# Transposing K, Q and memory rows in four 32-wide column tiles instead of one 128-wide tile

## The chip, the cores and the metric

The kernel runs on one core of a Trainium2 chip. The metric is the device time of one execution in microseconds; the figure for the kernel before is the median of 3 runs. A profile of one further execution shows where the time goes.

## What is computed

The output has two halves side by side. The left half (A) is a long convolution along the sequence, done with Fourier matrices. The right half (B), which takes most of the time and is where the change is, is attention with a recurrent memory. Cut to what matters:

```
mem = mem0                                   # 8 rows x 1024
for s in range(64):                          # 64 segments, one after the other
    h = concat(mem, x[32 rows of segment s]) # 40 rows x 1024
    q, k, v = h @ Wq, h @ Wk, h @ Wv         # 32 heads x 128 each
    p = softmax(mask(q k^T / sqrt(128)))     # 40 x 40 per head
    o = (p v) @ Wo                           # 40 rows x 1024
    mem = o[:8]                              # goes into the next segment
    out[s] = o[8:]
```

The memory rows of one segment are an input of the next, so the segments cannot overlap on the path through `mem`.

## The kernel before, in words

**Stages.** Up to about 450 us the kernel does half A, and beside it everything of B that does not depend on the memory. From then on it runs the 64 segments (loop at L884); one takes 22.5 us. Those 64 segments are the stage that the change touches.

**Weights.** Wk, Wq, Wv and Wo are cut into 64 chunks of 128 x 2048 bf16 (512 KB). 47 of them stay in SBUF. The other 17 (`STREAM`, L22) are read again from DRAM (tensor `WS`) in each segment, through a ring of tiles named `wring`. From the second segment on, one of the 17 is held in spare PSUM columns and is not read again, and of a second one only 192 KB are read (`KEPT`, L23). That leaves 15 full reads and one short one a segment. `done(ch)` (L834) gives a ring tile back when the last matmul that reads it has been written into the program, and `fetch()` (L716) issues the next read on SP's queue, at L724 or, for the short one, L721. A read waits until the tile it overwrites has been used; six ring tiles are in rotation.

**Order on TensorE.** The order is written out by hand (`tc.manual_schedule()`, L867); each engine works in program order. In one segment, L1020 to L1079:

- `fill_mem(hT, Y, 0)`, then half of the projection K of head group 0; `fill_mem(hT, Y, 1)`, then its other half. `Y` is the output of the segment before, as 128 x 512; `fill_mem` (L859) turns two 128 x 128 blocks of it on TensorE (L862) into PSUM, and VectorE copies the 8 memory columns of each from there into `hT` (L863), which is the weight operand of all projections.
- six projections (K, Q of group 0; K, Q of group 1; V of both groups), each as two calls of `Proj.run(4)`. One `run(4)` is 16 matmuls at L918: for each of four chunks, four matmuls with a 32-column weight (`hT`, 128 x 32) and 512 moving columns, at `tile_position=(0, 32*c)`. The four stand side by side in the array, each with 32 of its columns. After its second `run(4)` the sum is copied from PSUM to SBUF as bf16 by ScalarE (`evac`, L927, tile `qkv_sb`).
- `transposes(sb)` (L930) for K and Q of each group, four calls a segment (L1027, L1031, L1038, L1043). Each turns the four 128 x 128 blocks of `qkv_sb` (L933) into PSUM tile `tps`; VectorE copies the result for group 0, ScalarE for group 1. Each call stands between two `run(4)`, so that 16 projection matmuls lie between an `evac` and the transposes that read it; for the call of L1038, `scores(0)` lies there too.
- `scores` (L936): 32 matmuls with a 32-column weight and 40 moving columns each (L939, L942); softmax on VectorE and ScalarE; `attend` (L976) in 32-row tiles (L980, L984); `out_proj` (L1006) in 64-column tiles (L1002) into `yacc`.
- two ScalarE copies of `yacc` into the next `Y` (L1078), and two stores of its rows on POOL's queue (L1080).

"Tile form" below means the part of the array a matmul uses, as the profile prints it before the shapes: 128\*128 for the whole array, 128\*32 for a column tile of the projections and scores, 32\*128 for attend, 128\*64 for the output projection.

Of the kernel before, what the change touches and what calls it, by code (L numbers as in the profile page):

```python
# [416 lines left out]
def b_kernel(ctx: ExitStack, tc, x, mem0, Wq, Wk, Wv, Wo, outb, n_seg, run_a):  # L417
    nc = tc.nc
# [57 lines left out]
    ident = const.tile([128, 128], BF, name="ident")  # L476
# [262 lines left out]
    with c0p:  # L739
# [16 lines left out]
        for g in range(2):  # L756
# [3 lines left out]
            for tb in range(4):  # L760
                vst = vsts[:, tb] if g == 0 else pair()[:].rearrange("p (c w) -> p c w", c=4)
                for c in range(4):
                    ps = ps0.tile([128, 512], F32, tag="ps0", name="vb_ps")
                    for kc in range(8):
                        nc.tensor.matmul(ps[:], lhsT=xbt(kc)[:, 16 * tb:16 * tb + 16, :].rearrange("p s t -> p (s t)"),  # L765
                                         rhs=ws[kc][:, c * 512:(c + 1) * 512], start=(kc == 0), stop=(kc == 7))
# [87 lines left out]
    def load_x(s):  # L854
        rec = one.tile([128, 768], BF, tag="rec", name="rec")
        nc.gpsimd.dma_start(rec[:], REC[:, s, :])  # L856
        pend[s] = (rec[:, 0:256].rearrange("p (k t) -> p k t", k=8), rec[:, 256:512], rec[:, 512:768])

    def fill_mem(hT, Y, half):  # L859
        tp = tps[:, 0, :]  # L860
        for j in (2 * half, 2 * half + 1):
            nc.tensor.transpose(tp[:, j * 128:(j + 1) * 128], Y[:, j * 128:(j + 1) * 128], ident[:])  # L862
        nc.vector.tensor_copy(  # L863
            hT.rearrange("p (dh j) t -> p dh j t", dh=2)[:, :, 2 * half:2 * half + 2, 0:NM],
            tp.rearrange("p (j dh r) -> p dh j r", j=4, dh=2)[:, :, 2 * half:2 * half + 2, 0:NM])

    with tc.manual_schedule():  # L867
# [3 lines left out]
        Y = one.tile([128, 512], BF, tag="PT", name="Y0")  # L871
# [12 lines left out]
        for s in range(n_seg):  # L884
# [45 lines left out]
            def transposes(sb):  # L930
                tp = tps[:, 0, :]
                for i in range(4):
                    nc.tensor.transpose(tp[:, i * 128:(i + 1) * 128], sb[:, i * 128:(i + 1) * 128], ident[:])  # L933
                return tp.rearrange("p (i c r) -> p i c r", i=4, c=4)

            def scores(g, QT, KT):  # L936
# [79 lines left out]
            def out_quarter(q, w):  # L1016
                hp = [ch[1] for ch in kept if kept[ch] == "A"][0]
                project(2 * hp + q // 2, w, OT1)

            fill_mem(hT, Y, 0)  # L1020
            k0 = Proj(0, 0).run(4)
            fill_mem(hT, Y, 1)
            k0 = k0.run(4).evac()
            q0 = Proj(1, 0).run(4)
            KT0 = keys(0)
            last_queries(0)
            nc.vector.tensor_copy(KT0[:, :, :, 0:32], transposes(k0))  # L1027
            q0 = q0.run(4).evac()
            k1 = Proj(0, 1).run(4)
            QT0 = one.tile([128, 4, 4, 32], BF, tag="QT", name="QT")  # L1030
            nc.vector.tensor_copy(QT0[:], transposes(q0))  # L1031
            k1 = k1.run(4).evac()
            scores(0, QT0, KT0)
            E0 = softmax_a()
            q1 = Proj(1, 1).run(4)
            KT1 = keys(1)
            last_queries(1)
            nc.scalar.copy(KT1[:, :, :, 0:32], transposes(k1))  # L1038
            PT0 = softmax_b(E0)
            q1 = q1.run(4).evac()  # L1040
# [35 lines left out]
            Y = one.tile([128, 512], BF, tag="PT", name="Y")  # L1076
# [8 lines left out]
def kernel(  # L1085
# [27 lines left out]
    with ExitStack() as ctx_b:  # L1113
        b_kernel(ctx_b, tc, B_x[0], B_mem0[0],
                 B_Wq.rearrange("d h e -> d (h e)"), B_Wk.rearrange("d h e -> d (h e)"),
                 B_Wv.rearrange("d h e -> d (h e)"), B_Wo.rearrange("h e d -> (h e) d"),
                 outb, n_seg, run_a)
# [35 lines left out]
```

## Time and profile before

| | us |
|---|---|
| median of 3 runs (1904.03 to 1904.1) | 1904.04 |
| the profiled execution's own time | 1907.36 |
| its span, first to last instruction | 1905.6 |
| one segment, from the chain of waits | 22.51 |

| engine | busy in the span | share |
|---|---|---|
| TensorE matmuls (PE) | 1749.0 us, 26353 instructions | 92% |
| TensorE weight loads (PEld), beside the matmuls | 831.1 us, 26353 | 44% |
| VectorE (DVE) | 853.8 us | 45% |
| ScalarE (ACT) | 674.8 us | 35% |
| GpSimd (POOL) | 342.8 us | 18% |

How to read it: matmuls are pipelined, so the duration of one (380 ns for 512 columns) is longer than the time to the start of the next, and what a matmul costs is read from the starts. A number such as L933 is a line of the kernel. "x1024" counts instructions, and `out<-in` names the tile written and the tiles read. A wait is put down to the instruction whose semaphore ended it.

The transposes are 1024 matmuls at L933 and 256 at L862, each with 128 weight columns (the data) and 128 moving columns (the identity).

### The profile page before, as it was taken

Reading aid. Unit: us, or ns where it says so; the run is one execution under the profiler, and the core shown is the slowest. Engines: PE = TensorE matmul, PEld = TensorE weight load, DVE = VectorE, ACT = ScalarE, POOL = GpSimd, SP = SyncE. Lnnn points to the kernel's source line nnn. Section 1 sums busy time; section 2 is a strip of 40 time slices with the busy share of each in tenths; the row PEclk is TensorE's granted clock in tenths of the full one; section 3 lists DMA queues with packets and bytes.
Section 4 is the critical chain, followed back from the end, with each engine's and each line's share of the span. In section 5 each row is a group of like instructions: output and inputs, shape, how many; then the busy total and the mean of one; then the engine's idle time right before and its main releaser. Section 6 shows DMA issues by size and latency. Waiting matters only on the chain.

```text
span 1905.6 us, 62245 instructions
## 1 busy us (share of the span) xinstructions
PE 1749.0 (92%) x26353; PEld 831.1 (44%) x26353; DVE 853.8 (45%) x2812; ACT 674.8 (35%) x1195; POOL 342.8 (18%) x1014
## 2 busy tenths in 40 slices
PE   6989986778999999999999999999999999999998
PEld 3433322333444444444444444444444444444444
DVE  9927863202344444444444444444443444444443
ACT  6945640112333333333333333333333333333333
POOL 4003341000121111111121111111111111111111
PEclk9999998989999999999999999999999999999999
DMA  9989889998999999999999999999999999999998
GB/s 338 351 302 329 291 271 333 327 284 277 349 373 374 373 378 373 377 372 373 373 373 378 373 376 372 370 372 372 379 374 369 371 378 374 375 373 371 372 379 311
DMA packets 251211, 678.00 MB, mean 356 GB/s; under 512 B 74850, under 2 KB 82930, under 8 KB 250932
## 3 DMA queue, kind: packets, MB, share of 16 engines
q1 hardware_dynamic: 178692, 604.26, 85.0%
q0 software_dynamic: 17488, 46.70, 7.0%
q10 hardware_dynamic: 54752, 23.07, 4.5%
q8 instruction: 206, 3.38, 0.7%
q14 instruction: 73, 0.60, 0.1%
HBM read 618.35 MB, written 59.24 MB: 356 GB/s over the span
## 4 chain that ended last, share of the span: by engine, by line
PE 80%; DMA 7%; DVE 5%; issue 4%; ACT 2%; POOL 0%; ACTq 0%; SPq 0%; DVEq 0%; POOLq 0%
PE acc L918 38%; PE yacc L1002 22%; PE kb_ps L625 5%; PE tps L933 4%; DMA wring<-WS 3%; PE vb_ps L765 3%; DMA REC<-stage 2%; PE OTp L980 1%; ACT s_sb L243 1%; DVE rec L863 1%; PE SB L942 1%; PE tps L862 1%; PE s_ps L241 1%; DMA REC<-xt 1%; PE SB L939 1%
## 5 line engine op out<-in xcount | busy, mean ns | idle before, releaser
L918 PEld LDWEIGHTS <-rec 128*32 128x32 bf16 x12288 | 283.6, 96 | 300.2 <-DVE rec L863 60.7
L927 ACT CAST qkv_sb<-acc 128x512 bf16<-128x512 f32 x384 | 224.7, 585 | 480.0 <-PE acc L918 287.9
L1002 PEld LDWEIGHTS <-OT 128*64 128x64 bf16 x4348 | 255.1, 109 | 195.3 <-ACT OT L992 27.6
L918 PE MATMUL acc<-wring,rec 128*32 128x512 bf16 x2556 | 252.7, 382 | 22.8 <-DVE rec L863 19.1
L918 PE MATMUL acc<-Wres,rec 128*32 128x512 bf16 x3328 | 249.4, 380 | 0.6 <-issue 0.6
L1002 PE MATMUL yacc<-wring,OT 128*64 128x512 bf16 (+1 forms) x1540 | 235.9, 380 | 5.0 <-DMA wring<-WS 4.9
L918 PE MATMUL acc<-Wmid,rec 128*32 128x512 bf16 x3072 | 234.4, 382 | 0.0
L1002 PE MATMUL yacc<-Wmore,OT 128*64 128x512 bf16 (+1 forms) x1280 | 185.4, 381 | 0.0
L817 DVE TENSOR_SCALAR quarter<-OTp 128x256 int32<-128x256 int32 x252 | 101.1, 422 | 187.6 <-ACT OT L992 149.3
L1080 POOL DMA_DIRECT2D out_dram<-Y x128 | 63.7, 502 | 484.5 <-ACT Y L1078 484.2
L918 PE MATMUL acc<-pw,rec 128*32 128x512 bf16 x1796 | 144.8, 382 | 0.1
L1078 ACT CAST Y<-yacc 128x256 bf16<-128x256 f32 x128 | 41.4, 375 | 274.5 <-PE yacc L1002 274.5
L992 ACT CAST OT<-OTp 128x640 bf16<-128x640 f32 x128 | 88.6, 692 | 129.7 <-PE OTp L984 129.0
L918 PE MATMUL acc<-Wlate,rec 128*32 128x512 bf16 x1280 | 104.0, 384 | 17.1 <-DVE rec L863 17.1
L948 DVE TENSOR_REDUCE mx<-SB 128x5 f32<-128x200 f32 x128 | 47.1, 368 | 153.4 <-PE SB L942 153.3
L856 POOL DMA_DIRECT2D rec<-REC x64 | 36.2, 566 | 405.0 <-PE acc L918 372.1
L1002 PE MATMUL yacc<-Wlate,OT 128*64 128x512 bf16 x768 | 105.7, 383 | 0.2 <-ACT OT L992 0.2
L933 PEld LDWEIGHTS <-qkv_sb 128*128 128x128 bf16 x1024 | 57.8, 97 | 109.5 <-ACT qkv_sb L927 108.0
L933 PE MATMUL tps<-ident,qkv_sb 128*128 128x128 bf16 x1024 | 101.6, 222 | 0.4 <-ACT qkv_sb L927 0.3
L893 POOL COPY KT<-rec 128x128 bf16<-128x128 bf16 x128 | 38.2, 298 | 329.4 <-PE SB L942 324.2
L863 DVE COPY rec<-tps 128x32 bf16<-128x32 bf16 x128 | 22.3, 175 | 165.1 <-PE tps L862 115.8
L1027 DVE COPY KT<-tps 128x512 bf16<-128x512 bf16 x64 | 27.1, 424 | 152.2 <-PE tps L933 152.2
(215 smaller groups left out, 2392.9 us busy)
## 6 DMA issues: line engine op xcount, KB each, us to landing
wring<-WS SPq DMA_DIRECT2D x961, 512.0 KB, 6.0
rec<-REC POOLq DMA_DIRECT2D x64, 192.0 KB, 5.8
wring<-WS SPq DMA_DIRECT2D x63, 192.0 KB
SK<-s_sb SPq DMA_DIRECT2D x16, 512.0 KB, 4.8
SU<-s_sb SPq DMA_DIRECT2D x16, 512.0 KB, 4.9
Kg<-SK SPq DMA_DIRECT2D x32, 256.0 KB, 4.2
Ug<-SU SPq DMA_DIRECT2D x32, 256.0 KB, 5.7
REC<-stage ACTq DMA_DIRECT2D x16, 512.0 KB, 10.9
```

The costliest lines, as they stand in the source:

```text
L625: nc.tensor.matmul(ps[:], lhsT=ws[kc][:, hl * 128:(hl + 1) * 128], rhs=xbt(kc).rearrange("p s t -> p (s t)"), start=(kc == 0), stop=(kc == 7))
L765: nc.tensor.matmul(ps[:], lhsT=xbt(kc)[:, 16 * tb:16 * tb + 16, :].rearrange("p s t -> p (s t)"), rhs=ws[kc][:, c * 512:(c + 1) * 512], st ...
L817: nc.vector.tensor_scalar(out=t[:].bitcast(I32), in0=OTi[:, q, 160:416], scalar1=0, scalar2=None, op0=ALU.bitwise_or)
L863: nc.vector.tensor_copy(hT.rearrange("p (dh j) t -> p dh j t", dh=2)[:, :, 2 * half:2 * half + 2, 0:NM], tp.rearrange("p (j dh r) -> p dh ...
L918: nc.tensor.matmul(self.acc[32 * c:32 * c + 32, x - 512 * c:y - 512 * c], lhsT=hT[:, kc, :], rhs=r, start=(n_kc == 0 and x == 512 * c), st ...
L927: nc.scalar.copy(sb[:], self.acc[:])
L933: nc.tensor.transpose(tp[:, i * 128:(i + 1) * 128], sb[:, i * 128:(i + 1) * 128], ident[:])
L948: nc.vector.tensor_reduce(out=mx[:], in_=S, op=ALU.max, axis=AX.X)
L992: nc.scalar.copy(OT[:], o_view)
L1002: nc.tensor.matmul(yacc[64 * dh:64 * dh + m, x - o:y - o], lhsT=lhsT, rhs=r, start=(h == 0 and x == o), stop=(h >= 30), tile_position=(0, ...
L1078: nc.scalar.copy(Y[:, 256 * half:256 * half + 256], yacc[:, 256 * half:256 * half + 256])
L1080: nc.gpsimd.dma_start(bass.AP(outb.tensor, outb.offset + SEG * s * 2048 + 512 * dh, [[2048, 32], [1, 512]]), Y[64 * dh + NM:64 * dh + 40, :])
```

## The change

A helper `turn_tile` replaces each 128 x 128 transpose by four matmuls in transpose mode. Each takes 32 columns of the source as its weight, the whole identity as the moving operand, and writes 32 partitions of the result, at `tile_position=(0, e)`. Both places that transposed in the segment loop call it. Nothing else changes: the order on the other engines and the waits of the first instruction of each group are those of before.

```diff
+    def turn_tile(dst, src):
+        for e in range(0, 128, 32):
+            nc.tensor.matmul(dst[e:e + 32, :], lhsT=src[:, e:e + 32], rhs=ident[:], start=True, stop=True,
+                             is_transpose=True, tile_position=(0, e))
+
     def fill_mem(hT, Y, half):
         tp = tps[:, 0, :]
         for j in (2 * half, 2 * half + 1):
-            nc.tensor.transpose(tp[:, j * 128:(j + 1) * 128], Y[:, j * 128:(j + 1) * 128], ident[:])
+            turn_tile(tp[:, j * 128:(j + 1) * 128], Y[:, j * 128:(j + 1) * 128])
...
             def transposes(sb):
                 tp = tps[:, 0, :]
                 for i in range(4):
-                    nc.tensor.transpose(tp[:, i * 128:(i + 1) * 128], sb[:, i * 128:(i + 1) * 128], ident[:])
+                    turn_tile(tp[:, i * 128:(i + 1) * 128], sb[:, i * 128:(i + 1) * 128])
```

TensorE's 1280 transposes become 5120, each with its own weight load: 3840 more matmuls and 3840 more loads.

## The prediction

> **What bounds the kernel now.** I read the chain of waits first. In a segment it is TensorE almost from end to end; around one call of `transposes` it reads (start us, us, what):
>
> ```profile
> 1002.16 1.84 PE acc L918 x32
> 1004.00 0.33 PE tps L933 x4
> 1004.33 0.98 PE acc L918 x16
> ```
>
> So the transposes lie on the path, and a nanosecond saved on them is one on TensorE's path. What they really cost is read from starts. The timeline of another such call (start us, duration, engine, line, names, tile form and shapes; in brackets the idle time before and what ended it):
>
> ```profile
> 1001.06 0.58 ACT L927 CAST qkv_sb<-acc 128x512 bf16<-128x512 f32 x1 [3.10 <-issue]
> 1001.22 0.39 PE L918 MATMUL acc<-wring,rec 128*32 128x512 bf16 x4
> 1001.44 0.39 PE L918 MATMUL acc<-Wmid,rec 128*32 128x512 bf16 x4
> 1001.66 0.32 SPq L724 DMA_DIRECT2D wring<-WS  x1
> 1001.76 0.23 PEld L933 LDWEIGHTS <-qkv_sb 128*128 128x128 bf16 x4 [0.42 <-ACT qkv_sb L927]
> 1001.76 0.40 PE L933 MATMUL tps<-ident,qkv_sb 128*128 128x128 bf16 x4
> ...
> 1002.09 0.62 PE L918 MATMUL acc<-Wmid,rec 128*32 128x512 bf16 x8
> ```
>
> A group of four projection tiles starts 0.22 us after the one before (1001.22, 1001.44), but the first transpose starts 0.32 us after the last group. From the trace's stamps, the last projection matmul to the first transpose is 312 ns at the median of all 256 calls, against 215 inside a 512-column stream: 97 ns lost. The four transposes then start over 178 ns, and the next projection follows the last of them by 149 ns where transposes follow each other by 56: 93 ns lost. The first projection group after it takes 226 ns instead of 215: 11 more. Is this the change of tile form or the transpose itself? Two places answer. In the first stage a 128\*128 transpose is followed by a 128\*128 matmul:
>
> ```profile
> 278.29 0.23 PE L600 MATMUL xt_ps<-ident,X_sb 128*128 128x128 bf16 x1
> 278.36 0.59 PE L625 MATMUL kb_ps<-XBT,Wmid 128*128 128x512 bf16 x2
> ```
>
> Only 0.07 us lies between them. And the scores, in the same 128\*32 form as the projections, follow them without a loss:
>
> ```profile
> 1004.70 0.60 PE L918 MATMUL acc<-Wmid,rec 128*32 128x512 bf16 x8
> 1005.13 0.19 PE L939 MATMUL SB<-KT,QT 128*32 128x40 bf16 x4
> 1005.16 0.19 PE L942 MATMUL SB<-KT,QBm 128*32 128x40 bf16 x4
> ...
> 1005.38 0.41 PE L918 MATMUL acc<-pw,rec 128*32 128x512 bf16 x4
> ```
>
> 1004.70 to 1005.13 is two groups of 0.215 and nothing else, while the step into `attend` and those into the output projection, other forms, show 309 to 312 ns again. So the loss belongs to the change of form.
>
> The second thing to read is the DMA, from 500 to 1890 us: the rate in 40 equal slices, the queues' share of 16 engines' time, the ring's reads (count, size, median us to landing).
>
> ```profile
> GB/s 379 371 380 373 371 375 375 376 375 379 365 380 369 378 372 377 369 375 378 366 376 375 376 364 384 368 383 359 378 373 377 372 377 375 369 379 363 382 372 381
> ...
> q1 hardware_dynamic: 141904, 496.38, 95.0%
> q0 software_dynamic: 9856, 20.14, 4.3%
> ...
> wring<-WS SPq DMA_DIRECT2D x923, 512.0 KB, 6.0
> ```
>
> The queues add to 100% with the two instruction queues (1.1%). Yet TensorE hardly waits for it; its waits in that window (total us, times, longest):
>
> ```profile
> PE acc L918 <- DMA wring<-WS: 2.3, 4, 0.7
> ...
> PE yacc L1002 <- DMA wring<-WS: 0.3, 1, 0.3
> PE tps L933 <- ACT qkv_sb L927: 0.3, 2, 0.2
> ```
>
> 2.6 us in 1390. So TensorE sets the pace with the DMA close behind: of 939 reads whose landing and use can be paired in the trace, the median lands 1.97 us before its first matmul, one in ten less than 0.9, one in twenty less than 0.63.
>
> **The change, part by part.**
>
> *The transposes themselves.* The trace has no transpose in a column tile. The lower bound of four tiles on a 128 x 128 block is the stream of 128 columns side by side, 56 ns, as one 128-wide transpose now; nothing excludes that they run one after another, 4 x 56 = 224 ns. Rows near it: four projection tiles take 215 ns for 512 columns, which is one stream and not four; four score tiles, each with its own load, take 26 ns for 40 columns (32 in about 0.25 us). A form and column count between these rows, so I take 56 ns, and the 16 of a call 224 ns. Keep 224 a block for the range.
>
> *The loads.* Each tile brings a load. In the scores, 32 loads and 32 matmuls pass in 0.25 us, under 8 ns a pair, less than the 14 that 56/4 leaves. Cost: nothing, hidden behind the streams.
>
> [...]
>
> *Leaving a call.* From the first transpose to the next projection is now 178 + 149 = 327 ns, plus 11: 338. In one form it is 224. Saved 114, four times a segment: 456 ns.
>
> *Entering a call.* 97 ns go, but what is late next is `qkv_sb`. ScalarE's copy ends 115 ns before the first transpose for K of group 0 and 104 before both Qs; the shortest step from a ScalarE copy to a waiting matmul in this trace is 55 ns (Y at L1078 to L862). So these calls gain 60, 49 and 49. K of group 1 has `scores(0)` in front, its data is 377 ns early, and it gains the whole 97. Sum 255 ns.
>
> *Q of group 1 and the scores.* Leaving earlier brings the scores nearer to ScalarE's copy of QT: its end is now 181 ns ahead of them. Leaving gains 107 + 11 = 118, which leaves 63, still over 55. Cost nothing, with 8 ns of cover. The copies of group 0 on VectorE are shorter (424 against 587 ns) and have more.
>
> *`fill_mem`.* The first half waits for Y and then for VectorE: last transpose to projection is 542 ns, nearly all latency, and the form change hides in it: nothing. The second half enters from a projection with 312 ns and its data ready: 97 saved, and 10 on the spacing of the two (66 against 56); its exit waits for VectorE as before. 107 ns.
>
> Sum for TensorE: 456 + 255 + 107 = 818 ns a segment, 64 times: 52 us.
>
> *What the DMA gives back.* No part of the change touches its bytes: 374 GB/s x 22.515 us = 8.42 MB a segment. In 21.70 us that needs 388 GB/s. Two bounds. Above: no slice of the 40 (35 us each) is over 384; at 384 a segment takes 21.93 us, 0.585 less than now, 37 us in all. Below: shares that add to 100% say it is full already, and all 52 us turn into waits at L918 for `wring`. Against the lower end: reads land 1.97 us early, and over single segments the rate goes from 362 to 389. Against the upper: 389 is what the ring reaches when it catches up, and each read needs the slowest of 16 engines; in the median read the first engine lands after 3.8 us and the last after 6.0, so a thin margin is used up often. Neither row is nearer; I take the middle, 19 us, and keep both ends. Instruction fetch grows by 7680 instructions beside TensorE's 52706: at most 15% of that 1.1%, 0.16% of the DMA, some 3 us if the DMA is full, within this term.
>
> Sum: 1907.4 of the profiled execution less 19 is 1888.4; it lies 3.3 us above the median of the runs, so **1885 us**. The 52 us are found again as 33 us of waits for `wring`.
>
> **Rivals.**
>
> 1. *The DMA keeps up; all 52 us are kept*: 1904 − 52 = 1852. For it: 2.6 us of waits now and the 1.97 us of slack. Against it: 388 GB/s asked for over all segments.
> 2. *The DMA is full; nothing moves*: within 4 us of 1904. For it the 100%; then the waits for `wring` come to some 50 us.
> 3. *Slower: the four transpose tiles don't run side by side.* The place is L933 and L862 in every segment. Serial tiles cost 168 ns more a block, 20 blocks: 3.36 us, less 0.82, is 2.54 us a segment or 163 us: 2067 if whole. It decides from the spacing of a block: 818/20 = 41 ns above 56, so from about 97 ns a block the kernel is slower than before. Against it the projections and scores, which are side by side; for it only that transposes in this form occur nowhere.
> 4. *The change doesn't do what it says*: transpose mode beside plain matmuls in the 128\*32 form stalls as well. Then entering and leaving stay at 312 and 149 and the time is that of rival 2. Against it: 278.29 to 278.36 above.
>
> **How the numbers follow.** Partial gain (1862 to 1899): 0.55. Rival 1: 0.15. Rivals 2 and 4: 0.12. Rival 3: 0.18. The range leaves out rival 3, the top of 2 and the bottom of 1: 1850 to 1906, about 8 in 10. Faster by over 0.2%, about what a measurement of this kernel can tell from no change (1900.2), is partial gain and rival 1: 0.70; within it 0.12; slower 0.18.
>
> **What would show it.** Right: L933 and L862 in the 128\*32 form, a block every 56 ns; the step from L918 into a call 216 ns for K of group 1 and about 265 for the others; out of it under 60. The transposes' part of the chain falls from 0.33 to about 0.22 us a call. The DMA rate rises to about 379, and the ring's slack falls well below 1.97 us. Wrong: a block at 100 ns or more (rival 3); steps still at 312 and 149 (rival 4); waits for `wring` that stay at a few us (rival 1) or eat all (rival 2). The sum is wrong in its least certain term if the DMA's margin isn't near 0.3 us a segment.

## The result, and the profile after

| | us |
|---|---|
| before, median of 4 runs (1904.03 to 1908.61) | 1904.07 |
| after, median of 4 runs (1952.67 to 1959.26) | 1955.97 |
| ratio after / before, 95% interval | 1.0267 [1.0243, 1.0290] |
| forecast | 1885, range 1850 to 1906 |

The changed kernel is 52 us slower, and the forecast said 19 us faster. The granted TensorE clock was the same: 0.982 of full speed in the profiled execution of before, 0.982 to 0.984 in the four of after. The lines of the changed kernel have moved: the transposes are now at L861, the projections at L923, the scores at L944 and L947, attend at L985 and L989, the output projection at L1007.

The page of after: the span, the busy time of each engine, the queue that carries instructions (packets, MB, share of the DMA), and the chain of waits by engine.

```profile
span 1953.6 us, 69893 instructions
...
PE 1713.4 (88%) x30161; PEld 849.5 (43%) x30193; DVE 854.9 (44%) x2812; ACT 671.5 (34%) x1195; POOL 344.6 (18%) x1014
...
q8 instruction: 236, 3.87, 0.8%
...
PE 76%; issue 9%; DMA 7%; DVE 4%; ACT 2%; POOL 1%; ACTq 0%; SPq 0%; POOLq 0%; DVEq 0%
```

The two matching lines on the page of before:

```profile
q8 instruction: 206, 3.38, 0.7%
...
PE 80%; DMA 7%; DVE 5%; issue 4%; ACT 2%; POOL 0%; ACTq 0%; SPq 0%; DVEq 0%; POOLq 0%
```

TensorE is busy for less time than before (1713 against 1749 us), and its share of the chain falls. What grew is "issue", from 4 to 9%: time in which an engine stood still and waited for nothing that the profile shows.

**The transposes became as cheap as forecast.** The timeline of TensorE around one call that met no disturbance (start us, duration, engine, line, operation, names, tile form, shapes):

```profile
1043.95 0.40 PE L923 MATMUL acc<-pw,rec 128*32 128x512 bf16 x4
1044.16 0.41 PE L861 MATMUL tps<-ident,qkv_sb 128*32 128x128 bf16 x16
1044.39 0.40 PE L923 MATMUL acc<-pw,rec 128*32 128x512 bf16 x4
```

The call begins 0.21 us after the last group of projections, the ordinary step inside a stream, and the next projection follows its first transpose by 0.23 us, where before it was 0.327. The spacing of blocks, read from the stamps, is 56 ns at the median, as with the 128-wide transpose.

**The loss stands elsewhere, as holes.** The chain of waits of after through the next call (start us, us, what):

```profile
1043.46 0.89 PE acc L923 x16
1044.35 0.22 PE tps L861 x16
1044.57 1.73 PE acc L923 x32
1046.30 0.10 PE tps L861 x2
1046.40 0.85 issue
1047.25 0.40 PE tps L861 x14
```

The call at 1044.35 is whole. The one at 1046.30 stops after two of its 16 transposes, stands for 0.85 us, and goes on. No semaphore is waited for in the middle of a call. The waits of TensorE in the segment stage of after, from 500 to 1940 us (total us, times, longest):

```profile
PE acc L923 <- DVE rec L868: 37.7, 122, 0.3
PE tps L861 <- ACT Y L1083: 28.7, 62, 0.5
PE acc L923 <- issue: 27.1, 32, 1.4
PE tps L861 <- issue: 13.9, 13, 1.7
PE SB L947 <- issue: 9.1, 9, 1.4
PE SB L944 <- issue: 8.5, 8, 2.1
PE OTp L985 <- issue: 7.7, 7, 1.6
...
PE acc L923 <- DMA wring<-WS: 0.9, 2, 0.5
```

The same list of before, from 500 to 1890 us:

```profile
PE acc L918 <- DVE rec L863: 35.4, 120, 0.4
PE tps L862 <- ACT Y L1078: 28.8, 62, 0.5
...
PE acc L918 <- issue: 0.6, 1, 0.6
```

The first two lines of each are the waits at the start of a segment. The lines with "issue" of after add up to 71 us with the two smaller ones left out above; in before there was 0.6 us of them. They fall on every kind of matmul, the unchanged ones too, and the longest is 2.1 us. The wait that the forecast feared, for the weight ring `wring`, is 0.9 us here.

**What the holes wait for.** I numbered TensorE's instructions in the trace of after: a matmul with its weight load is two, and each of its 145 semaphore instructions is one. From 490 us on there are 86 holes of over 0.43 us between two matmuls, those at the head of a segment, where it waits for `Y` and then for VectorE, left out (before: 7). 82 of them end 1 to 1.8 us behind a packet of queue q8 (before: 2, one of them at a border). 81 of the 82 stand at number 192, 193 or 194 modulo 256. A packet of q8 is 16 KB (3.87 MB / 236), and there are 30 more packets for 7680 more instructions: 256 instructions each. By these counts TensorE gets its instructions in blocks of 256, and I read the holes as the places where one block ends and the next is not there yet. All that stand between 1000.2 and 1095 us, in us ("border before" is where the block before began):

```
border before   packet of q8         last start   goes on   hole    after the packet
1000.21         1002.78 - 1003.86    1004.69      1005.14   0.46    1.28
1015.04         1018.25 - 1019.32    1019.69      1020.68   0.99    1.36
1020.68         1023.34 - 1024.42    1024.85      1025.62   0.77    1.20
1041.95         1044.61 - 1045.64    1046.17      1047.25   1.07    1.61
1062.13         1064.52 - 1065.78    1066.62      1067.23   0.61    1.45
1067.23         1069.69 - 1070.76    1071.26      1072.17   0.91    1.41
1088.18         1091.83 - 1092.92    1092.41      1094.26   1.85    1.34
```

Read the fourth row, which is the hole of the chain above. At 1041.95 a block began. The packet with the next one set out only at 1044.61, 2.66 us later, and was in at 1045.64. TensorE ran the 256 instructions of its block in 4.22 us and stood from 1046.17 on. It went on 1.61 us after the packet's end. The last column is the tell-tale: whatever TensorE was to do next, it resumes 1.2 to 1.6 us after a packet.

So a block needs, by the stamps of before: 2.4 us at the median from the border to the packet's start (0.4 to 4.6), 1.03 us for the packet, and 1.2 to 1.6 us from its end to the first instruction (the least in any kernel here is 1.16), together 4.6 to 5.0 us; "4.7 us" below stands for this. And a stretch of 256 instructions lasts: in before never under 5.33 us. In after it lasts as little as 4.03. That is what the edit did, and it can be worked out. Scores are 64 instructions in 0.25 us, a call of transposes is now 32 instructions in 0.22 us, and a group of four projections is 8 in 0.215. A stretch with two calls and one `scores` had 16 + 64 instructions in 0.65 + 0.25 us, and 176 more of projections in 22 x 0.215 = 4.7 us: 5.6 us. Now it has 64 + 64 in 0.45 + 0.25 us and 128 more in 16 x 0.215 = 3.4 us: 4.1 us. Only the second is under 4.7.

**The balance.** From the first to the last start of a segment (63 of them) before takes 1487.1 us and after 1532.6: 45.5 us more. (Of the rest of the 52 us, 1.8 falls into the last segment, and 3.3 is what the profiled execution of before lies above the median of its runs.) How much TensorE gained and how much it stood still, the experiments take apart.

### The profile page after: what moved, and what is told of

It reads as the page before. It is cut to its first block, busy times and chain, and to the rows that moved or that the text cites. A ratio compares the mean times of both kernels' runs of the same rounds, so it can differ in the third digit from the quotient of the medians.

```text
span 1953.6 us, 69893 instructions
## 1 busy us (share of the span) xinstructions
PE 1713.4 (88%) x30161; PEld 849.5 (43%) x30193; DVE 854.9 (44%) x2812; ACT 671.5 (34%) x1195; POOL 344.6 (18%) x1014
## 3 DMA queue, kind: packets, MB, share of 16 engines
q8 instruction: 236, 3.87, 0.8%
## 4 chain that ended last, share of the span: by engine, by line
PE 76%; issue 9%; DMA 7%; DVE 4%; ACT 2%; POOL 1%; ACTq 0%; SPq 0%; POOLq 0%; DVEq 0%
PE acc L923 36%; PE yacc L1007 22%; PE tps L861 4%; PE kb_ps L625 4%; PE vb_ps L765 3%; DMA wring<-WS 2%; DMA REC<-stage 2%; PE OTp L985 1%; DVE rec L868 1%; ACT s_sb L243 1%; PE SB L947 1%; PE SB L944 1%; PE s_ps L241 1%; DMA zt<-SZ 1%; PE ks_ps L279 1%
## 5 line engine op out<-in xcount | busy, mean ns | idle before, releaser
L923 PEld LDWEIGHTS <-rec 128*32 128x32 bf16 x12288 | 302.6, 96 | 312.9 <-DVE rec L868 61.9
L1007 PEld LDWEIGHTS <-OT 128*64 128x64 bf16 x4348 | 256.0, 109 | 199.0 <-issue 26.7
L923 PE MATMUL acc<-wring,rec 128*32 128x512 bf16 x2556 | 258.0, 381 | 29.4 <-DVE rec L868 20.6
L923 PE MATMUL acc<-Wres,rec 128*32 128x512 bf16 x3328 | 260.5, 380 | 19.8 <-issue 19.0
L1007 PE MATMUL yacc<-wring,OT 128*64 128x512 bf16 (+1 forms) x1540 | 237.4, 380 | 4.7 <-DMA wring<-WS 4.0
L923 PE MATMUL acc<-Wmid,rec 128*32 128x512 bf16 x3072 | 232.6, 379 | 0.0
L1007 PE MATMUL yacc<-Wmore,OT 128*64 128x512 bf16 (+1 forms) x1280 | 185.5, 381 | 0.0
L923 PE MATMUL acc<-pw,rec 128*32 128x512 bf16 x1796 | 147.4, 381 | 5.2 <-issue 4.1
L861 PE MATMUL tps<-ident,qkv_sb 128*32 128x128 bf16 x4096 | 109.0, 221 | 14.3 <-issue 13.9
L923 PE MATMUL acc<-Wlate,rec 128*32 128x512 bf16 x1280 | 103.9, 384 | 18.1 <-DVE rec L868 18.1
L861 PEld LDWEIGHTS <-qkv_sb 128*32 128x32 bf16 x4096 | 69.6, 96 | 98.3 <-ACT qkv_sb L932 67.8
L1007 PE MATMUL yacc<-Wlate,OT 128*64 128x512 bf16 x768 | 107.1, 383 | 2.7 <-issue 1.7
L625 PE MATMUL kb_ps<-XBT,pw 128*128 128x512 bf16 x313 | 84.5, 402 | 9.8 <-ACT stage L614 5.9
```

Of the source, the lines that this page charges most:

```text
L625: nc.tensor.matmul(ps[:], lhsT=ws[kc][:, hl * 128:(hl + 1) * 128], rhs=xbt(kc).rearrange("p s t -> p (s t)"), start=(kc == 0), stop=(kc == 7))
L861: nc.tensor.matmul(dst[e:e + 32, :], lhsT=src[:, e:e + 32], rhs=ident[:], start=True, stop=True, is_transpose=True, tile_position=(0, e))
L923: nc.tensor.matmul(self.acc[32 * c:32 * c + 32, x - 512 * c:y - 512 * c], lhsT=hT[:, kc, :], rhs=r, start=(n_kc == 0 and x == 512 * c), st ...
L1007: nc.tensor.matmul(yacc[64 * dh:64 * dh + m, x - o:y - o], lhsT=lhsT, rhs=r, start=(h == 0 and x == o), stop=(h >= 30), tile_position=(0, ...
```

## The experiments

The theory: late blocks of instructions. Three rivals: A, the DMA is full and the kernel is bound by its bytes; B, transposes in column tiles stall TensorE by themselves; C, only the number of instructions counts, not where they stand.

The extra matmuls of some kernels write 8 columns of the PSUM tile of the scores, and change the scores of the kernels that have them. They are these, called where each diff shows:

```diff
+        def idle(n):
+            for j in range(n):
+                c = 32 * (j % 4)
+                nc.tensor.matmul(SB[c:c + 32, 256:264], lhsT=ident[:, c:c + 32], rhs=ident[:, 0:8], start=True,
+                                 stop=True, skip_group_check=True, tile_position=(0, c))
```

All ratios are to the kernel before, run on the same chip, with their 95% intervals.

### Half the bytes, without and with the change

From the second segment on only the first 1024 columns of a streamed chunk are read, and are used for the other 1024 too. TensorE's instructions stay the same; half_before is the kernel before with this edit, half_after the changed kernel.

```diff
+            elif s > 0:
+                nc.sync.dma_start(t[:, 0:1024], stream_src(ch)[:, 0:1024])
...
-        return [(0, 2048, live[now[0], ch][1][:])]
+        t = live[now[0], ch][1]
+        if now[0] > 0 and ch not in kept:
+            return [(0, 1024, t[:, 0:1024]), (1024, 2048, t[:, 0:1024])]
+        return [(0, 2048, t[:])]
```

> The kernel before, but from the second segment on each full ring read fetches only the first 1024 of its 2048 columns, and the matmuls of the second half use the first half again, so part of the weights is wrong. The DMA moves about half as much in the segments. My theory of the result: TensorE runs out of instructions, because blocks of 256 of them (the 16 KB packets of the instruction queue, 206 before and 236 after, a difference of 30 = 7680/256) land late behind the ring's reads. The kernel before does not suffer from it, so with less DMA it stays at 1895 to 1905 us. Rival A, that the ring's bandwidth already bounds the kernel before: clearly faster, under 1880.

Measured: 1902.15 us, 0.9989 [0.9979, 0.9999]. Half the bytes free the kernel before of next to nothing; A falls.

> The changed kernel with the same half-length ring reads (second half of each streamed weight wrong). Theory of late instruction blocks: with the DMA half empty the blocks land in time, the waits of TensorE for no visible cause (71 us in the segments of the changed kernel) go, and the 52 us of the prediction come out: 1845 to 1860 us, below the kernel before. Rival B, that the transposes in column tiles themselves stall TensorE now and then, whatever the DMA does: it stays within 15 us of 1955.

Measured: 1853.94 us, 0.9729 [0.9715, 0.9744]. The same TensorE instructions that lose 52 us with the full ring gain 50 with half of it; B falls. TensorE's waits in half_after, 500 to 1840 us, and the ring's reads and the rate in 40 slices, 500 to 1800 us:

```profile
PE acc L928 <- DVE rec L873: 37.8, 122, 0.3
PE tps L866 <- ACT Y L1088: 28.2, 61, 0.5
PE OTp L994 <- issue: 0.3, 1, 0.3
```

```profile
GB/s 204 211 205 212 205 212 205 207 205 207 205 207 207 210 206 208 207 210 205 210 205 209 206 210 206 210 206 211 203 211 206 211 205 209 206 208 206 209 206 203
...
wring<-WS SPq DMA_DIRECT2D x895, 256.0 KB, 3.1
```

The rows with "issue" come to 1.0 us in place of 71. They are gone although the stretches are as short as in after, 4.03 us at the least: the supply has become faster. A packet of q8 starts 0.6 us after the border at the median in half_before, and 1.05 in half_after, where with the full ring it is 2.4 (before) and 2.75 (after); the packet itself takes 0.97 to 0.98 against 1.02 to 1.05. With 1.2 us more to the first instruction a block needs some 3.2 us in half_after. So in these runs it takes both: dense instructions, and a DMA that is busy with something else (late blocks: 81 in after with both, 1 in before and 2 in half_after with one of them, none in half_before).

The pair also splits the balance. The 63 segments take 1482.5 us in half_before and 1435.2 in half_after: TensorE gained 47.3 us, 0.75 a segment (22.51 to 21.74 at the median, 0.77). From half_after to after, with the same instructions, it is 97.4 us. The 81 holes at block borders, less the 60 ns that lie between two such matmuls anyway, add up to 96.4 us in the trace of after. (The list of waits has only 71 us of "issue" because it counts from the modelled end of the matmul before and puts a few of the holes down to other engines; here a hole is counted from start to start.) So 47 us gained and 97 lost; with the 4.6 us that half the bytes save in before, 97.4 - 47.3 - 4.6 gives the 45.5 of the balance.

### More instructions in the kernel before, in dense places and in a wait

The transposes stay as before; 60 small matmuls are added to each segment, as many as the change adds. paddense has them 15 each after the calls for k0, q0 and q1 and before `scores(0)`:

```diff
             nc.vector.tensor_copy(KT0[:, :, :, 0:32], transposes(k0))
+            idle(15)
...
             nc.vector.tensor_copy(QT0[:], transposes(q0))
+            idle(15)
...
+            idle(15)
             scores(0, QT0, KT0)
...
             nc.scalar.copy(QT1[:], transposes(q1))
+            idle(15)
```

> The kernel before with its 128-wide transposes, and 60 tiny extra matmuls (8 columns, 32-column tiles, into spare PSUM columns, nothing reads them) in each segment: 15 after the transposes of K and Q of group 0 and Q of group 1 and 15 ahead of the first scores. That is as many extra instructions as the change adds, in the same part of the segment, without its transposes. At the scores' 6.5 ns each they cost 0.4 us a segment, 25 us. Theory of late instruction blocks: stalls come on top, 1960 to 2020 us in all, with TensorE idle for no visible cause in the dense part. Rival B: 1925 to 1935.

Measured: 1975.02 us, 1.0364 [1.0349, 1.0380]. Its waits from 500 to 1940 us:

```profile
PE acc L924 <- issue: 14.9, 19, 1.6
PE SB L885 <- issue: 4.4, 7, 0.8
PE tps L939 <- issue: 2.7, 3, 1.7
```

The small matmuls themselves cost 0.4 us a segment (the shortest segment is 22.93 us against 22.51), 26 us in all; its 63 segments take 63 us more than those of before, and the rest is late blocks: 42 holes at numbers 193 and 194. No column-tile transpose is in this kernel, and the holes are there. padwait has the same 60 at the head of the segment, where TensorE waits for `Y` anyway:

```diff
+            idle(60)
             fill_mem(hT, Y, 0)
```

> The kernel before and 60 tiny extra matmuls (8 columns, into spare PSUM columns of the scores' bank, so the scores are disturbed) in each segment, all ahead of the first half of fill_mem, where TensorE waits 0.46 us for Y anyway. As many extra instructions as the change adds, but in a wait. Theory that the time of a stretch of 256 instructions decides, against the 4.7 us a block takes to arrive: no stretch in the dense part gets shorter, the fastest stays 4.8 us, 1904 to 1918. Rival C, that only the total number of instructions fetched counts: 1950 or more.

Measured: 1906.43 us, 1.0008 [0.9999, 1.0017], with 2 late blocks. As many instructions as in after (30193 weight loads), and no loss: C falls. What counts in these runs is the shortest time that 256 instructions in a row take (4.79 us here, 4.03 in after), not their number.

### The change with fewer instructions around it

few_scores is the changed kernel with two of the 32 scores matmuls of each `scores` kept; the other 30 are left out, so its scores are not those of the reference. It has 26353 matmuls, as before had.

```diff
-                        nc.tensor.matmul(S[32 * c:32 * c + 32, i, :], lhsT=QT[:, i, c, :], rhs=KT[:, i, c, :],
-                                         start=False, stop=False, skip_group_check=True, tile_position=(0, 32 * c))
-                    for c in range(4):
-                        nc.tensor.matmul(S[32 * c:32 * c + 32, 4, :], lhsT=QBm[:, c, i, :], rhs=KT[:, i, c, :],
...
+                        if i == 0 and c < 2:
+                            nc.tensor.matmul(S[32 * c:32 * c + 32, i, :], lhsT=QT[:, i, c, :], rhs=KT[:, i, c, :],
+                                             start=False, stop=True, skip_group_check=True,
+                                             tile_position=(0, 32 * c))
```

> The changed kernel without 60 of the 64 score matmuls of a segment (all of the own-memory queries, and 14 of 16 of the others), so the scores are wrong; the ring reads are whole. It has as many TensorE instructions as the kernel before, with all transposes in column tiles, and what is left out is in the dense part. Theory of late instruction blocks: the waits without a visible cause nearly go; the 52 us come out and the scores' 0.4 us a segment besides, some 1827, with the DMA now as the next bound: 1825 to 1875 us. Rival B (column-tile transposes stall by themselves): stalls stay, 1915 to 1935.

Measured: 1832.82 us, 0.9615 [0.9600, 0.9631]. All of the change's transposes at the full ring, and no loss. It also answers the forecast's question on the DMA. The rate from 500 to 1800 us with the ring's queue (packets, MB, share of 16 engines), and TensorE's waits from 500 to 1820 us:

```profile
GB/s 396 399 392 394 396 399 396 399 393 400 393 395 395 395 391 390 396 389 388 394 395 395 398 397 397 396 396 396 393 397 399 391 393 395 399 395 397 394 397 396
...
q1 hardware_dynamic: 140152, 490.36, 96.9%
```

```profile
PE acc L923 <- DVE rec L868: 38.5, 124, 0.4
PE tps L861 <- ACT Y L1081: 28.6, 62, 0.5
PE acc L923 <- issue: 1.3, 3, 0.6
```

395 GB/s over 1300 us, more than any slice of before, and no wait for `wring` in TensorE's list.

### Moving the borders

shift85 adds 85 small matmuls once, in the second segment, to move every later border of a block by 170 instructions.

```diff
+            if s == 1:
+                idle(85)
             fill_mem(hT, Y, 0)
```

> The kernel before, with 85 tiny extra matmuls (8 columns, into spare PSUM columns, nothing reads them) once, ahead of the second segment, hidden in its wait for Y: under 1 us by themselves. In the kernel before a segment is exactly 384 matmuls and 384 loads, three blocks of 256 instructions, so the block boundaries fall at the same three places in each segment; its fastest boundary-to-boundary stretch takes 5.9 us. After the shift one stretch starts in the scores and takes 4.8 us. Theory of late instruction blocks (a block takes 5.0 to 6.8 us to arrive in the changed kernel): a stall of 0.3 to 0.9 us in each of 63 segments, 1920 to 1960 us. Rival B (column-tile transposes stall) and the view that only the number of instructions counts: 1904 to 1906.

Measured: 1905.11 us, 1.0000 [0.9991, 1.0010]: a miss of the theory's number. I had taken the borders to stand still in the segment, since 384 matmuls are three blocks of 128. They don't: the 145 semaphore instructions, about two a segment, are in the blocks as well, and the borders drift by one matmul a segment. In before a border passes from matmul 99 of a segment (the fifth) to 42 (the sixty-second). Moved by 85 matmuls, most stretches are still long: 16 of 184 are under 5.0 us (shortest 4.77), and only one block was late. A block arrives in about 4.7 us at the median, so those were on the edge and not past it. The miss is one of geometry, and the run says little for or against the theory.

### One tile fewer for the ring

ring5 is the changed kernel with five tiles in the ring instead of six, so that less is under way in the DMA at once.

```diff
-            if now[0] == 0 and i == LATE_SLOT:
-                free.append(2)
-                fetch()
```

> The changed kernel with five ring tiles in rotation instead of six, so one read less is queued at the DMA. If an instruction block waits behind the ring reads that are queued ahead of it, it now arrives earlier than 4.7 us after its predecessor is begun, and the waits without a visible cause shrink; waits for the ring grow, since reads are issued 1.4 us later against a slack of some 2 us: 1915 to 1950 us. If a block takes turns with the ring whatever is queued: no shorter, and the time stays at 1950 to 1985.

Measured: 2016.28 us, 1.0578 [1.0544, 1.0612], beyond both expectations. The waits from 500 to 1940 us:

```profile
PE tps L858 <- DVE wring L800: 58.8, 60, 1.0
PE acc L920 <- DVE rec L865: 35.5, 116, 0.4
PE acc L920 <- issue: 21.5, 23, 1.7
PE yacc L1004 <- DMA wring<-WS: 19.4, 31, 2.2
```

The late blocks stay (70 of them; the packet starts 2.56 us after the border at the median, against 2.75 in after), and two new waits come on top. Either the depth of the ring is not what delays the packet, or one tile is too little to show it; the run can't tell which.

### Parts of the change that pay

fill_only has column tiles in `fill_mem` alone, k0_only in the call for K of group 0 alone, fill_k0 in both. All three compute the whole reference.

```diff
+            def transposes(sb, tiled=False):
...
+                    if tiled:
+                        turn_tile(tp[:, i * 128:(i + 1) * 128], sb[:, i * 128:(i + 1) * 128])
+                    else:
+                        nc.tensor.transpose(tp[:, i * 128:(i + 1) * 128], sb[:, i * 128:(i + 1) * 128], ident[:])
...
+            nc.vector.tensor_copy(KT0[:, :, :, 0:32], transposes(k0, True))
```

> Only the memory rows (fill_mem) are transposed in column tiles; K and Q in one 128-wide tile as before. 12 more instructions a segment for each half, in the thin part of the segment. Prediction's own sum: 107 ns a segment, 6.8 us less. Theory of late blocks: hardly any new stall, 1896 to 1902. Rival B: 24 column-tile transposes a segment bring a fifth to a third of the changed kernel's stalls, 1910 to 1930.

(It has 16 column-tile transposes a segment.) Measured: 1900.25 us, 0.9979 [0.9968, 0.9991].

> Only the transposes of K of group 0 are in column tiles, 24 more instructions a segment, in the part before the first scores, where a stretch of 256 instructions takes 5 us or more. Prediction's own sum: 174 ns a segment, 11 us less. Theory of late blocks: a few us of stalls, 1893 to 1904. Rival B: a quarter of the changed kernel's stalls, 25 us, so 1915 to 1920.

Measured: 1900.34 us, 0.9974 [0.9964, 0.9985], with 12 late blocks.

> Memory rows and K of group 0 transposed in column tiles, the other three calls 128 wide: the two parts that gained alone, together. If gains add (65 ns of fill_mem and 165 ns of K a segment, by the shortest segments of the two runs) and the thin part of the segment takes the 36 more instructions with few late blocks: 1890 to 1899 us, the best of all with a right output. If late blocks already eat it: 1900 to 1906.

Measured: 1897.47 us, 0.9955 [0.9941, 0.9968]: faster than both kernels by its interval, if by little. Its waits from 500 to 1880 us:

```profile
PE acc L923 <- DVE rec L868: 38.2, 123, 0.4
PE tps L861 <- ACT Y L1086: 28.6, 62, 0.5
PE acc L923 <- issue: 2.7, 7, 0.9
PE SB L950 <- issue: 1.1, 3, 0.5
```

TensorE gains 0.23 us a segment (22.51 to 22.28 for the shortest), 14 us in all, and about half of it goes again at some 11 late blocks. Little of the gain is left because the margin was small: each instruction that is added shortens the stretch around it.

The runs in one table. Stretch: time of 256 TensorE instructions, the shortest and the 5th percentile. Tight: share of blocks that begin less than 1.6 us after the end of their packet. Late: holes at the border of a block. Segment: median.

```
kernel        stretch us      tight   late   segment us   time us    ratio
before        5.33   5.51     0.06     1     22.51        1904.07
half_before   5.33   5.49     0.00     0     22.51        1902.15    0.9989
padwait       4.79   5.01     0.08     2     22.52        1906.43    1.0008
shift85       4.77   4.85     0.10     1     22.52        1905.11    1.0000
fill_only     4.79   5.03     0.10     2     22.45        1900.25    0.9979
fill_k0       4.79   5.15     0.21    11     22.29        1897.47    0.9955
k0_only       4.79   5.00     0.19    12     22.35        1900.34    0.9974
few_scores    4.71   4.96     0.11     3     21.30        1832.82    0.9615
paddense      3.68   4.41     0.34    42     23.55        1975.02    1.0364
after         4.03   4.63     0.48    81     23.32        1955.97    1.0267
ring5         3.99   4.23     0.39    70     24.21        2016.28    1.0578
half_after    4.03   4.22     0.10     2     21.74        1853.94    0.9729
```

The stretch of a late block has the hole at its end in it, so the rows of paddense, after and ring5 look longer than the instructions make them: half_after, with the instructions of after and hardly a hole, has 90 of 215 stretches under 4.7 us. Without the holes, over the ten kernels with the full ring, about 70% of the 229 stretches under 4.7 us ended in a late block, about 16% of the 244 between 4.7 and 5.3 us, and 1 to 2% of the 1533 above. So late blocks become the rule below some 4.7 us, which is the time that a block needs at the median, and a few come above it, since the packet's start varies from 0.4 to 4.6 us; with half the bytes, 4.03 us are still enough.

## Why the prediction was wrong

**The step that failed** is one sentence of the DMA's part: "Instruction fetch grows by 7680 instructions beside TensorE's 52706: at most 15% of that 1.1%, 0.16% of the DMA, some 3 us if the DMA is full, within this term." It priced the fetch by its bytes. The bytes are indeed nothing (q8 has 0.8% of the DMA). What counted is how long TensorE had to wait for the next 256 instructions (4.7 us), against how long the last 256 kept it busy (as little as 4.03 us). That step cost 97 us in place of 3, which turned the 47 us gained into the loss, and no rival had it. Both numbers for it could have been looked for in before: the stamps of q8's packets against TensorE's instruction count, with 6% of the blocks of before already beginning within 1.6 us of their packet's end. And one block of before was late already.

Point by point, with half_after for TensorE's side because hardly anything there is late (2 blocks):

- *The loss belongs to the change of form.* Right. In half_after the step into the call for K of group 1, whose data is early, is 191 ns, where 312 stood before, and the exit from a call 30 to 47 ns, where 149 stood.
- *Transposes at 56 ns a block, side by side.* Right: 56 ns at the median, and the four tiles of a block start 3 ns apart in three of the calls and 8 in the one for K of group 1. Rival 3 falls.
- *The loads cost nothing.* Right in TensorE's time: a block with its four loads takes 56 ns in half_after. Where the price stood is that each load and each matmul is an instruction in a packet of q8: 7680 more of them, and 30 more packets.
- *Leaving: 224 ns from the first transpose to the next projection.* 234 in three calls and 223 in the one for K of group 1.
- *Entering: the first transpose 55 ns behind ScalarE's copy.* 53 ns in the three calls concerned.
- *`fill_mem`, second half: 107 ns.* 106 of the entry came (312 to 206), but the way from its first transpose to the projection grew by 16 ns (552 to 568), and in the first half by 24 (608 to 632), so some 66 were left. fill_only agrees: 22.51 to 22.45. The sum then closes: 818 less 41 here, less 10 at each of three exits, plus 24 that the entry of K of group 1 gained beyond its 97, is 771 ns, and a segment is 770 ns shorter.
- *The sum for TensorE, 52 us.* 47 over the 63 segments, right but for that.
- *The DMA gives back 33 us, since 388 GB/s are too near the top.* Wrong, and a second error in the same direction as the measured loss, though not its cause: with half the ring's bytes the kernel before takes 0.9989 of its time (half_before), so the DMA was no bound, and few_scores carries 395 GB/s with no wait for `wring`. The 384 of the best slice was what the kernel asked for, not what the DMA could do, and shares that add up to 100% did not mean that it was full. Rival 1 had the better reading of the DMA; half_after's 1854 is its 1852, under a condition that it did not name.
- *What would show it.* The list in the forecast looked for waits for `wring` in TensorE's list. "issue" wasn't in it.

In before one block of some 180 was late; in after 81 of some 210 were, and cost 97 us. Why a packet starts 0.4 to 4.6 us after the border under the full ring, and what happens in the 1.2 us and more between its end and the first instruction, no run here takes apart.

## What to carry to other kernels

Before an edit that puts more and smaller instructions in a dense place, find the shortest time that 256 of them in a row take, and hold it against the time from border to first instruction of a block (here 4.7 us under a loaded DMA). Well above it (here from 5.3 us on) the instructions were nearly free (1 to 2% late); below it most blocks were late (about 70%), and each cost 1.2 us (96.4 us over 81 of them in after). When the chain shows "issue" in the middle of a group that waits for nothing, number the engine's instructions and look at the holes modulo 256. And shares that add up to 100% did not mean here that the DMA was full (half the ring's bytes took 0.1% off the kernel before): look for something that waits for it.

## What the runs showed of the hardware

- Late blocks: in after TensorE resumes 1.20 to 1.61 us after the end of the packet at all 81 of them; with the DMA at 207 GB/s the packets start about 1 us after the border (half_after) instead of 2.75 (after).
- TensorE's semaphore instructions are in the blocks too: 145 of them move the borders by a matmul a segment, from matmul 99 in the fifth to 42 in the sixty-second (before).
- Transposes in four 32-wide column tiles run side by side: 3 to 8 ns between the tiles of a block, 56 ns a block (half_after).
- The DMA moved 395 GB/s through 1300 us with its shares adding up to 102%, and TensorE's list of waits has none for the ring (few_scores).
